# One RWKV and PReLU kernel: u loaded on its own queue, fills and the token table moved to GpSimd, the check of alpha moved back

## The chip, the cores and the metric

The kernel runs on one core of a Trainium2 chip. The core has five engines with an instruction stream each: TensorE (PE; its weight loads are shown as PEld), VectorE (DVE), ScalarE (ACT), GpSimd (POOL) and SyncE (SP, which issues most of the DMAs). They wait for one another by semaphores. The metric is the time of one execution on the device, in microseconds (us); less is better.

## The reference, cut to what matters

An attention-like recurrence for 4 batches, 8 heads, 768 tokens and a head size of 48, and behind it a two-layer network with a leaky activation whose slope `alpha` is a number for each of 2048 inner features:

```python
state = zeros(B, H, D, D)
for t in range(S):
    cur = einsum('bhd,bhe->bhde', u[None] * kt, vt)
    y[:, :, t] = einsum('bhd,bhde->bhe', rt, state + cur)
    state = w[None, :, :, None] * state + einsum('bhd,bhe->bhde', kt, vt)
x = y.transpose(0, 2, 1, 3).reshape(B * S, H * D)
h = x @ w_in                                   # (3072, 384) @ (384, 2048)
out = (maximum(h, 0) + alpha * minimum(h, 0)) @ w_out
```

All tensors are float32. The decay `w` lies between 0.85 and 0.95.

## The kernel before, in words

**Chunks and pairs.** The 768 tokens are cut into six chunks of 128. The recurrence is done chunk by chunk, two heads (a "pair") at a time: four pairs q = 0 to 3 in each chunk. Within a chunk the products of r and k (the scores), masked to earlier tokens, stand for the recurrence; r and k are first multiplied by powers of the decay from a table W[q] (a scan of w and a reciprocal, L275 and L278). What passes from a chunk to the next is a state T[q].

**The first chunk** (`first_chunk`). For each pair: two loads (r and k, 224 KB each), two products with the table on VectorE (L447), scores on TensorE (L457, in two PSUM banks), the diagonal term with u (product L533 on VectorE, sums L540 on TensorE, L464 for v times these sums), masks that keep the part above the diagonal (`below`; for the first of two banks by a predicated copy on VectorE, L477, and for the second by a copy on ScalarE, L471, and a select on GpSimd, L473), and y on TensorE (L485 and L489). y goes to SBUF by ScalarE (L504) in a coarse and a fine part, with a correction matmul between (L508); pairs 1 to 3 also take up a piece of pair 0's heads (L498). The state needs k by tokens times a table: `tokens_table` makes eight pieces of 112x64 (L315, two for each pair), transposes them on TensorE (L322), copies the result (`whalf`, L325), scales k with it (L431), and L521 makes the product.

**Chunks 1 to 5** (`prepare`, `burst`). The same in a denser form, at set steps of the network. Here the diagonal goes into the scores' mask itself: `base` holds for each of 2 heads and 4 batches a 64x64 identity times a sum `cu`, and VectorE copies the scores over its upper part (L681). In chunk 1 (called hasty) these eight fills for each pair are GpSimd operations (L594), later ones ScalarE copies (L598). TensorE's bursts are L626, L633, L652 and L662.

**The network** runs in 96 steps, 16 blocks of 128 inner features for each chunk: nine matmuls in (L740), the activation on ScalarE and VectorE (L748, L749, L752, L753), nine matmuls out (L774), some steps later. Weights come packed and are unpacked once into a coarse and a fine part, wh and wl, by ScalarE and VectorE (L359, L362, L365, L374, L377, L378).

**The check** (`check`, L813 to L829) counts whether all alpha are at most 1 and w is in a range; SyncE and the others read the flag and branch to a slow general path if not.

**What sets the order.** A planner (`Plan.in_order`) takes all pieces with an estimated duration, what they read and write, and a rank. It walks through time with its own estimates and gives each engine the ready piece of lowest rank. The engines then run their streams in that order, so a rank or an estimate that is changed moves instructions. Where the plan leaves TensorE idle before the first output matmul, filler matmuls on the identity are put in (`warm`, L834); 19 more stand at the start of the program. Loads are in the same order on SyncE's queue, the first r on ScalarE's (L420). Buffers and five PSUM banks are given out in the same walk.

## Time and profile before

| | |
|---|---|
| median of 3 runs | 485.31 us (484.8 to 485.47) |
| profiled execution | 485.77 us |
| its span, first to last instruction | 483.7 us |
| TensorE busy | 473.4 us (98%) |
| VectorE busy | 309.9 us (64%) |
| ScalarE busy | 244.8 us (51%) |
| GpSimd busy | 98.4 us (20%) |
| mean granted TensorE clock | 0.998 |

The shares are means over two stages. In the first 80 us the first two chunks and the unpacking of the weights run beside the first steps of the network, and VectorE and ScalarE are busy most of the time; after that the network's matmuls follow one another. Busy times of TensorE are those of pipelined matmuls, whose ends are modelled, so what one piece of work takes is better read from the start of its first matmul to the start of the next piece.

### The profile page before, as it was taken

To read this page: it belongs to the slowest core of one execution; us is meant where nothing else is said; L and a number is where in the kernel's file an instruction comes from. 1 tells how busy PE (TensorE), PEld (TensorE's weight loads), DVE (VectorE), ACT (ScalarE), POOL (GpSimd) and SP (SyncE) were. 2 spreads that over 40 slices of the span, in tenths; PEclk is the share of its full clock that TensorE was granted. 3 is DMA by queue.
4 is the path that set the end of the run, shared out by engine and by line. 5 is a ranking of instruction groups with operands and counts; after the bars stand their busy time and mean duration, and the time that the engine had idled before them with its cause. 6 is when DMAs were issued, how large, how long until landed. Compare 5 with 4: busy or idle time off the path is not lost.

```text
span 483.7 us, 11271 instructions
## 1 busy us (share of the span) xinstructions
PE 473.4 (98%) x4667; PEld 385.5 (80%) x4667; DVE 309.9 (64%) x519; ACT 244.8 (51%) x554; POOL 98.4 (20%) x119
## 2 busy tenths in 40 slices
PE   8999999999999999999999999999999999999994
PEld 6777777888888888888888888888888878888883
DVE  6999899999777774864754865754553543333330
ACT  3877897766555553553552653553642342423332
POOL 5119890012414030411201402200200000000000
PEclk9999999999999999999999999999999999999999
DMA  7975885641154631521211421210400000100002
GB/s 220 284 228 184 250 248 170 214 147 51 54 160 122 211 96 59 149 88 37 88 54 37 151 89 35 72 56 1 119 1 1 1 1 0 66 0 1 0 0 71
DMA packets 23113, 46.22 MB, mean 96 GB/s; under 512 B 3376, under 2 KB 11184, under 8 KB 23056
## 3 DMA queue, kind: packets, MB, share of 16 engines
q1 hardware_dynamic: 21968, 43.24, 28.5%
q0 software_dynamic: 960, 1.97, 2.0%
q8 instruction: 38, 0.62, 0.5%
q10 hardware_dynamic: 128, 0.23, 0.2%
q14 instruction: 19, 0.16, 0.1%
HBM read 37.17 MB, written 6.29 MB: 90 GB/s over the span
## 4 chain that ended last, share of the span: by engine, by line
PE 86%; DVE 5%; POOL 4%; ACT 2%; DMA 2%; issue 1%; ACTq 0%; DVEq 0%
PE acc L774 40%; PE bank L740 38%; POOL base L594 4%; PE bank L652 2%; PE bank L662 2%; PE bank L633 2%; PE bank L626 1%; DMA raw<-rk 1%; DVE raw L447 1%; ACT x L717 1%; DVE raw L565 1%; DMA wp<-wP 1%; DVE wl L378 1%; DVE kk L431 0%; DVE g L533 0%
## 5 line engine op out<-in xcount | busy, mean ns | idle before, releaser
L740 PE MATMUL bank<-x,wh 128*128 128x512 f32 x576 | 195.3, 392 | 0.0
L749 DVE SCALAR_TENSOR_TENSOR g<-bank,alph,g 128x512 f32<-128x512 f32 x96 | 71.9, 749 | 106.6 <-ACT g L748 106.5
L740 PEld LDWEIGHTS bank<-x,wh 128*128 128x128 f32 x576 | 108.1, 188 | 24.0 <-issue 0.8
L748 ACT ACTIVATE g<-bank 128x512 f32<-128x512 f32 x96 | 57.2, 596 | 129.2 <-PE bank L740 128.8
L740 PE MATMUL bank<-x,wl 128*128 128x512 f32 x288 | 112.2, 389 | 0.0
L752 ACT ACTIVATE gh<-g 128x512 fp32r<-128x512 f32 x96 | 60.5, 630 | 72.2 <-DVE g L749 72.1
L753 DVE TENSOR_TENSOR gl<-g,gh 128x512 fp32r<-128x512 f32 x96 | 72.4, 754 | 36.9 <-ACT gh L752 36.8
L774 PE MATMUL acc<-gh,wh 128*128 128x512 f32 x288 | 83.2, 396 | 0.0
L774 PE MATMUL acc<-gh,wl 128*128 128x512 f32 x288 | 81.6, 390 | 0.0
L774 PE MATMUL acc<-gl,wh 128*128 128x512 f32 x288 | 81.5, 390 | 0.0
L774 PEld LDWEIGHTS acc<-gh,wl 128*128 128x128 f32 x288 | 53.9, 188 | 11.4
L774 PEld LDWEIGHTS acc<-gl,wh 128*128 128x128 f32 x288 | 53.9, 188 | 11.3
L740 PEld LDWEIGHTS bank<-x,wl 128*128 128x128 f32 x288 | 54.1, 188 | 10.8
L774 PEld LDWEIGHTS acc<-gh,wh 128*128 128x128 f32 x288 | 52.7, 188 | 11.6 <-issue 0.4
L582 POOL TENSOR_TENSOR rr<-rr,kk 128x384 f32<-128x384 f32 x16 | 22.3, 1393 | 161.4 <-DMA kk<-vkr 93.6
L598 ACT ACTIVATE base<-ident,cu 128x64 f32<-128x64 f32 x128 | 32.9, 337 | 1.7 <-DVE cu L588 1.7
L594 POOL TENSOR_SCALAR base<-ident,cu 128x64 f32<-128x64 f32 x32 | 30.8, 984 | 13.7 <-ACT cu L546 13.7
L390 POOL DMA_DIRECT2D x<-x x30 | 15.4, 519 | 61.3 <-ACT o L801 49.4
L406 DVE TENSOR_TENSOR x<-bank,x 48x256 fp32r<-48x256 f32 x64 | 27.0, 422 | 1.3
L405 ACT ACTIVATE x<-bank 48x256 fp32r<-48x256 f32 x64 | 24.2, 379 | 2.1 <-PE bank L662 1.0
L568 DVE TENSOR_TENSOR raw<-raw,W 112x512 f32<-112x512 f32 x32 | 22.4, 723 | 2.2 <-DMA raw<-rk 2.2
L584 POOL TENSOR_TENSOR rr<-rr,utab 128x384 f32<-128x384 f32 x16 | 22.5, 1408 | 1.2
(116 smaller groups left out, 395.8 us busy)
## 6 DMA issues: line engine op xcount, KB each, us to landing
wraw<-wall SPq DMA_DIRECT2D x15, 768.0 KB, 4.7
raw<-rk SPq DMA_DIRECT2D x45, 224.0 KB, 3.9
v<-vkr SPq DMA_DIRECT2D x24, 192.0 KB, 3.4
kk<-vkr SPq DMA_DIRECT2D x20, 192.0 KB, 3.6
rr<-vkr SPq DMA_DIRECT2D x16, 192.0 KB, 2.5
oT<-o SPq DMA_DIRECT2D x12, 256.0 KB, 2.2
x<-x POOLq DMA_DIRECT2D x30, 64.0 KB, 2.7
oT<-g SPq DMA_DIRECT2D x6, 256.0 KB, 4.3
```

Of the source, the lines that this page charges most:

```text
L405: add("ACT", us, lambda: nc.scalar.activation(h(), view(), AF.Copy), r=[src], w=parts(x, 0, ps), rank=rank)
L406: add("DVE", us + 0.1, lambda: nc.vector.tensor_tensor(out=l(), in0=view(), in1=h(), op=ALU.subtract), r=[src] + parts(x, 0, ps), w=parts( ...
L568: add("DVE", 0.72, lambda t=t, tab=tab: nc.vector.tensor_tensor(out=t().rearrange("p b (j t) -> p (b j) t", j=2), in0=t().rearrange("p b ( ...
L584: add("POOL", 1.2, lambda: nc.gpsimd.tensor_tensor(out=rt().rearrange("p (g b) e -> p g b e", g=2), in0=rt().rearrange("p (g b) e -> p g b ...
L594: add("POOL", 1.0, lambda g=g, b=b: nc.gpsimd.tensor_scalar(base()[:, g, b], ident2(), cu()[:, g, b:b + 1], None, op0=ALU.mult), r=[cu, id ...
L598: add("ACT", 0.32, lambda g=g, b=b: nc.scalar.activation(base()[:, g, b], ident2(), AF.Copy, scale=cu()[:, g, b:b + 1]), r=[cu, ident2], w ...
L740: nc.tensor.matmul(hp()[:, :], a[i]()[:, k], X[c]()[:, x, k], start=(k == 0 and j == 0), stop=(k == NK - 1 and j == 2))
L748: add("ACT", 0.6, lambda: nc.scalar.activation(g(), hp()[:, :], AF.Copy), r=[hp], w=[g], rank=n - 100)
L749: add("DVE", 0.75, lambda: nc.vector.scalar_tensor_tensor(out=g(), in0=hp()[:, :], scalar=alph()[:, i:i + 1], in1=g(), op0=ALU.mult, op1=A ...
L752: add("ACT", 0.64, lambda: nc.scalar.activation(gh(), g(), AF.Copy), r=[g], w=[gh], rank=n - 100)
L753: add("DVE", 0.73, lambda: nc.vector.tensor_tensor(out=gl(), in0=g(), in1=gh(), op=ALU.subtract), r=[g, gh], w=[gl], rank=n - 99)
L774: nc.tensor.matmul(banks[k](), a[i]()[:, NK + k], x(), start=(begin and j == 0), stop=(end and j == 2))
```

## The change

Seven things are edited.

- u is loaded from ScalarE's queue, ahead of the first r, instead of from SyncE's; w stays first on SyncE's. The planner counts small loads with a fixed time.
- The four operations that square the last element of the table into `w128` (L279) go from VectorE to GpSimd.
- For pairs 0 and 1 of the first chunk both banks are masked by a ScalarE copy and a GpSimd select, where the first bank was a predicated copy on VectorE. The two memsets that those copies needed fall away, and the planner's estimate of a select goes from 1.6 to 0.75.
- The eight pieces of the token table (L315) go from ScalarE to GpSimd; the transposes behind them (L322) get a lower rank.
- The diagonal fills of all later chunks, eight small operations for each pair, on GpSimd in chunk 1 and on ScalarE afterwards, become two GpSimd selects of 64x512 that read `cu` with a step of zero.
- The check moves from step 40 to step 24, and two of its operations now also read the last weight tile, so they can't run before the weights are unpacked.
- 16 filler matmuls instead of 19 at the start, and none in the gap right behind them.

```diff
-                dma = max(dma, p.end + 1.5) + p.kb / DMA_RATE
-                p.end = dma + 0.3
+                if p.kb < 16:
+                    p.end += 1.7
+                else:
+                    dma = max(dma, p.end + 1.5) + p.kb / DMA_RATE
+                    p.end = dma + 0.3
...
-    load(up, lambda: nc.sync.dma_start(up(), uP), 1, -98.95)
+    add("ACT", 0.45, lambda: nc.scalar.dma_start(up(), uP), w=[up], rank=-111, kb=1)
...
-        for g in range(2):
-            if g == 0:
-                add("POOL", 0.4, lambda i=i, g=g: nc.gpsimd.memset(below[i][g](), 0.0), w=[below[i][g]], rank=-95 + i)
...
-        add("DVE", 0.1, lambda: nc.vector.tensor_tensor(
+        add("POOL", 0.25, lambda: nc.gpsimd.tensor_tensor(
             out=w128()[:, m:m + 1], in0=t()[:, 128:129], in1=t()[:, 128:129], op=ALU.mult), r=[t], w=[(w128, m)],
             rank=10 * m - 78)
...
-                add("ACT", 0.3, lambda m=m, j=j: nc.scalar.activation(
-                    rows()[:, m, HI * j:HI * (j + 1)], W[m]()[:, L - 1:HI - 1:-1], AF.Copy,
-                    scale=w128()[:, m:m + 1] if first and j == 0 else W[m]()[:, L:L + 1]),
+                add("POOL", 0.5, lambda m=m, j=j: nc.gpsimd.tensor_scalar(
+                    rows()[:, m, HI * j:HI * (j + 1)], W[m]()[:, L - 1:HI - 1:-1],
+                    w128()[:, m:m + 1] if first and j == 0 else W[m]()[:, L:L + 1], None, op0=ALU.mult),
                     r=[W[m], (w128, m)], w=[(rows, (m, j))], rank=at)
...
-        add("PE", 0.6, turn, r=[rows, ident], w=[pt], rank=at)
+        add("PE", 0.6, turn, r=[rows, ident], w=[pt], rank=at - 49 * first)
...
-            if g and True:
-                add("ACT", 0.6, lambda: nc.scalar.activation(
-                    base[1]().rearrange("p b t -> p (b t)"), A[1]()[:, :], AF.Copy), r=[A[1]], w=[base[1]], rank=q - 94)
-                add("POOL", 1.6, lambda: nc.gpsimd.affine_select(
-                    base[1](), base[1](), pattern=[[0, B], [1, L]], base=0, channel_multiplier=-1,
-                    compare_op=ALU.is_gt, fill=0.0), w=[base[1]], rank=q - 94)
+            if g or q < 2:
+                add("ACT", 0.6, lambda g=g: nc.scalar.activation(
+                    base[g]().rearrange("p b t -> p (b t)"), A[g]()[:, :], AF.Copy), r=[A[g]], w=[base[g]], rank=q - 94)
+                add("POOL", 0.75, lambda g=g: nc.gpsimd.affine_select(
+                    base[g](), base[g](), pattern=[[0, B], [1, L]], base=0, channel_multiplier=-1,
+                    compare_op=ALU.is_gt, fill=0.0), w=[base[g]], rank=q - 94)
                 continue
...
-        for g in range(2):
-            for b in range(B):
-                if hasty:
-                    add("POOL", 1.0, lambda g=g, b=b: nc.gpsimd.tensor_scalar(
-                        base()[:, g, b], ident2(), cu()[:, g, b:b + 1], None, op0=ALU.mult), r=[cu, ident2],
-                        w=[(base, (g, b))], rank=at - 0.9)
-                    continue
-                add("ACT", 0.32, lambda g=g, b=b: nc.scalar.activation(
-                    base()[:, g, b], ident2(), AF.Copy, scale=cu()[:, g, b:b + 1]), r=[cu, ident2],
-                    w=[(base, (g, b))], rank=at - 0.9)
+        for j in range(2):
+            rows = slice(HI * j, HI * (j + 1))
+            add("POOL", 0.75, lambda rows=rows: nc.gpsimd.affine_select(
+                base()[rows].rearrange("p g b t -> p (g b) t"),
+                cu()[rows].rearrange("p g b -> p (g b)")[:, :, None].broadcast_to([HI, 2 * B, HI]),
+                pattern=[[0, 2 * B], [1, HI]], base=0, channel_multiplier=-1, compare_op=ALU.is_equal, fill=0.0),
+                r=[cu], w=[base], rank=at - 0.9)
...
-        at = 40
+        at = 24
...
-        add("DVE", 0.1, lambda: nc.vector.tensor_scalar(ok()[:, 0:NF], alph(), 1.0, None, op0=ALU.is_le), r=[alph],
+        add("DVE", 0.1, lambda: nc.vector.tensor_scalar(ok()[:, 0:NF], alph(), 1.0, None, op0=ALU.is_le), r=[alph, wl[NF - 1]],
...
-    add("PE", 4.0, lambda: [warm() for _ in range(19)], r=[ident], w=[(bank, "warm")], rank=-1000)
+    add("PE", 3.4, lambda: [warm() for _ in range(16)], r=[ident], w=[(bank, "warm")], rank=-1000)
...
-    tokens_table(L, True, -45)
+    tokens_table(L, True, -44)
```

The order of the instructions moves in many places, of which three matter below. In it, line numbers of the changed kernel differ by a few from those before (L322 and L457 are the same in both, L740 is L737, L834 is L831).

**VectorE, its first operations behind the memsets.** `W_95`, `W_96` and `W_97` are the tables of pairs 0, 1 and 2, `raw` is r or k. Before:

```order
L275 SCALAR_TENSOR_TENSOR W_95<-wp,unit 112x65
L278 RECIPROCAL W_95<-W_95 112x64
L447 TENSOR_TENSOR raw<-raw,W_95 112x512 x2
L533 TENSOR_TENSOR g<-raw 112x512
L275 SCALAR_TENSOR_TENSOR W_96<-wp,unit 112x65
L278 RECIPROCAL W_96<-W_96 112x64
```

And in the changed kernel:

```order
L275 SCALAR_TENSOR_TENSOR W_95<-wp,unit 112x65
L278 RECIPROCAL W_95<-W_95 112x64
L275 SCALAR_TENSOR_TENSOR W_96<-wp,unit 112x65
L278 RECIPROCAL W_96<-W_96 112x64
L447 TENSOR_TENSOR raw<-raw,W_95 112x512
L275 SCALAR_TENSOR_TENSOR W_97<-wp,unit 112x65
L447 TENSOR_TENSOR raw<-raw,W_95 112x512
L533 TENSOR_TENSOR g<-raw 112x512
```

Pair 1's table and the scan of pair 2's now stand ahead of pair 0's second product.

**GpSimd, from u's products to chunk 1.** `below` and `gl` are the masked scores of even and odd pairs, `g` in L315 is the token table. Before:

```order
L270 TENSOR_TENSOR uw<-up,wp 48x4 x2
L473 AFFINE_SELECT below_136<-below_136 128x512
L473 AFFINE_SELECT gl<-gl 128x512
L473 AFFINE_SELECT below_136<-below_136 128x512
L473 AFFINE_SELECT gl<-gl 128x512
L594 TENSOR_SCALAR base<-ident_90,cu 128x64 x16
```

And in the changed kernel, from pair 1's selects on:

```order
L473 AFFINE_SELECT gl<-gl 128x512 x2
L315 TENSOR_SCALAR g<-W_95,w_99 112x64
L473 AFFINE_SELECT below_136<-below_136 128x512
L315 TENSOR_SCALAR g<-W_95 112x64
L315 TENSOR_SCALAR g<-W_96,w_99 112x64
L315 TENSOR_SCALAR g<-W_96 112x64
L315 TENSOR_SCALAR g<-W_97,w_99 112x64
L315 TENSOR_SCALAR g<-W_97 112x64
L473 AFFINE_SELECT gl<-gl 128x512
L315 TENSOR_SCALAR g<-W_98,w_99 112x64
L315 TENSOR_SCALAR g<-W_98 112x64
L593 AFFINE_SELECT base<-cu 64x512 x4
```

The eight pieces of the table stand among the selects of pairs 2 and 3, and the fills of chunk 1 are four instructions where 16 were.

**TensorE, around the token table's transpose.** Behind pair 2's y, whose bank is `bank_142` before and `bank_143` afterwards, there stood:

```order
L498 MATMUL bank_142<-x_338,pick 128x512 x2
L485 MATMUL bank_146<-ident,gh 128x128 x4
L489 MATMUL bank_146<-gl,v 48x128 x8
L498 MATMUL bank_146<-x_338,pick 128x512 x2
L508 MATMUL bank_142<-x,less_138 128x512
L322 MATMUL bank_144<-ident,g 128x112 x4
```

And now, from the correction of pair 1 (`bank_142`) on:

```order
L508 MATMUL bank_142<-x,less_138 128x512
L322 MATMUL bank_146<-ident,g 128x112 x4
L498 MATMUL bank_143<-x_345,pick 128x512 x2
L485 MATMUL bank_144<-ident,gh 128x128 x4
L489 MATMUL bank_144<-gl,v 48x128 x8
L508 MATMUL bank_143<-x,less_138 128x512
L498 MATMUL bank_144<-x_345,pick 128x512 x2
```

L322 now stands ahead of the rest of pairs 2 and 3.

## Rows read from the trace of the kernel before

**Rows 1.** Table by stretch: stretch, its us, busy us per engine (x), PEclk, DMA.

```profile
30.69:80.00 49.31, 48.05 (x771) 36.53 (x770) 45.18 (x72) 40.75 (x86) 37.84 (x40) 1.00 0.71 221
80.00:476.67 396.67, 396.66 (x3578) 327.36 (x3576) 238.01 (x393) 184.43 (x420) 53.06 (x54) 1.00 0.22 68
```

**Rows 2.** Timeline of TensorE, start: start us, us, instruction, [idle before <-releaser].

```profile
1.46 5.09 PE L834 MATMUL acc<-ident 128*128 128x256 bf16 x23 [1.46 <-POOL ident L249]
6.48 1.55 PE L457 MATMUL bank<-raw 48*128 48x128 f32 x16
...
8.52 0.83 PE L834 MATMUL acc<-ident 128*128 128x256 bf16 x6
9.28 1.16 PE L457 MATMUL acc<-raw 48*128 48x128 f32 x16
...
12.67 0.39 PE L834 MATMUL acc<-ident 128*128 128x256 bf16 x2
13.25 1.16 PE L457 MATMUL bank<-raw 48*128 48x128 f32 x16 [0.19 <-DVE raw L447]
```

**Rows 3.** Timeline of TensorE, 16.9 to 64 us.

```profile
16.92 0.73 PE L498 MATMUL bank<-x,pick 112*128 112x512 f32 x2
...
21.27 0.73 PE L498 MATMUL bank<-x,pick 112*128 112x512 f32 x2
...
25.15 0.39 PE L834 MATMUL acc<-ident 128*128 128x256 bf16 x2
25.69 0.60 PE L303 MATMUL bank<-ident,raw 112*128 112x112 f32 x4 [0.16 <-DVE raw L565]
...
30.69 0.82 PE L834 MATMUL acc<-ident 128*128 128x256 bf16 x6
31.50 0.67 PE L521 MATMUL bank<-v,kk 128*64 128x48 f32 x16
32.40 0.63 PE L540 MATMUL bank<-uw,g 112*64 112x2 f32 x16 [0.24 <-DVE g L533]
...
43.64 0.59 PE L652 MATMUL bank<-raw,T 48*48 48x64 f32 x26 [0.34 <-DVE base L681]
...
63.09 0.66 PE L652 MATMUL bank<-raw,T 48*48 48x64 f32 x32 [0.69 <-ACT x L717]
```

**Rows 4.** Timeline of VectorE, its first operations on the table.

```profile
3.73 0.29 DVE L275 TENSOR_TENSOR_SCAN W<-wp,unit 112x65 f32<-112x65 f32 x1 [2.60 <-DMA wp<-wP]
4.06 0.55 DVE L278 RECIPROCAL W<-W 112x64 f32<-112x64 f32 x1
4.64 1.32 DVE L447 TENSOR_TENSOR raw<-raw,W 112x512 f32<-112x512 f32 x2
```

**Rows 5.** DMA issues: queue, count, KB, us from issue to landing.

```profile
raw<-rk ACTq DMA_DIRECT2D x1, 224.0 KB, 3.3
```

**Rows 6.** Timeline of VectorE: a mask of the first chunk.

```profile
18.23 0.73 DVE L477 COPY_PREDICATED below<-strict,bank 128x512 f32<-128x512 uint8 x1
```

**Rows 7.** Line L594 on GpSimd; the timeline of GpSimd and VectorE beside its longest.

```profile
L594 POOL TENSOR_SCALAR base<-ident,cu x32: 433/442/4077, 34.0 to 66.1; 128x64 f32<-128x64 f32 x32
54.56 4.08 POOL L594 TENSOR_SCALAR base<-ident,cu 128x64 f32<-128x64 f32 x1
55.03 0.95 DVE L374 SCALAR_TENSOR_TENSOR wx<-wraw,wx 128x768 uint32<-128x768 uint32 x1
...
57.37 0.95 DVE L378 TENSOR_TENSOR wl<-wx,wh 128x768 fp32r<-128x768 f32 x1
```

**Rows 8.** Timeline of GpSimd and VectorE: a select, and the product beside it.

```profile
8.81 0.64 POOL L473 TENSOR_SCALAR_AFFINE_SELECT below<-below 128x512 f32<-128x512 f32 x1 [2.78 <-ACT below L471]
8.85 1.14 DVE L533 TENSOR_TENSOR g<-raw 112x512 f32<-112x512 f32 x1
...
13.23 0.69 DVE L533 TENSOR_TENSOR g<-raw 112x512 f32<-112x512 f32 x1
```

**Rows 9.** Table by stretch, TensorE alone, behind its last matmul.

```profile
476.70:481.70 5.00, 0.00 (x0) 1.00 0.46 166
```

More of the change, by code (lines that the diff above doesn't have):

```diff
@@ L811, in check @@
         count = psum()
-        at = 40
+        at = 24
         add("POOL", 0.1, lambda: (ok(), w2(), nc.gpsimd.memset(ok()[:, 0:NF + P], 0.0)), w=[ok], rank=at)
-        add("DVE", 0.1, lambda: nc.vector.tensor_scalar(ok()[:, 0:NF], alph(), 1.0, None, op0=ALU.is_le), r=[alph],
+        add("DVE", 0.1, lambda: nc.vector.tensor_scalar(ok()[:, 0:NF], alph(), 1.0, None, op0=ALU.is_le), r=[alph, wl[NF - 1]],
             w=[ok], rank=at)
-        add("DVE", 0.1, lambda: nc.vector.tensor_tensor(out=w2(), in0=wp(), in1=wp(), op=ALU.mult), r=[wp], w=[w2],
+        add("DVE", 0.1, lambda: nc.vector.tensor_tensor(out=w2(), in0=wp(), in1=wp(), op=ALU.mult), r=[wp, wl[NF - 1]], w=[w2],
             rank=at)
@@ L858, in rwkv_prelu_kernel @@
         jobs.append((n + MLAG - 0.5, 5, lambda n=n: m_out(n)))
-    jobs.append((40, 7, check))
+    jobs.append((24, 7, check))
     for m in range(P):
@@ L878, in rwkv_prelu_kernel @@
             step = p.rank >= 0 and p.us == 0.7
-            fill[p], last = 0 if last is None else int(max(0.0, p.start - last - 0.05) / (0.25 if step else 0.125)), p.end
+            fill[p] = 0 if last is None else int(max(0.0, p.start - last - 0.05) / (0.25 if step else 0.125))
+            last = p.end if p.rank > -1000 else None
     with tc.manual_schedule():
```

## The prediction

> **What bounds the kernel now.** I read the table of busy time by stretch first. From 80 us to the last matmul at 476.67 TensorE has 0.01 us without work, and between 30.69 and 80 it lacks 1.26 us (49.31 less 48.05) [rows 1]. The matmuls that count are the same ones in both programs: the listed order has every kind in the same number, and only the filler matmuls of L834 drop from 39 to 20. So from 80 us on nothing can be won, whatever the other engines do, and the time moves only by what TensorE wastes before. The next view is TensorE's timeline. The waste is, in order: 6.48 us until the first scores, of which 23 fillers fill 5; two fillers at 12.67 with an idle bit behind (0.58 us to the next piece) [rows 2]; two at 25.15 (0.54 to 25.69), six at 30.69 (0.81 to 31.50), and idle time of 0.24, 0.34 and 0.69 us before L540 and L652 [rows 3]. Behind the start that is 3.2 us together. It is the whole prize, under 0.7%, and it is also all the cover: a new wait of TensorE in this stage is paid in full.
>
> **The change, part by part.** The profiled execution took 485.77 us, 2.07 more than its span of 483.7; the median of the runs is 485.31. I work out a difference in the profiled execution and put it on the median.
>
> *The start.* The first scores (L457) wait for r and k of pair 0 times the table. Before, VectorE needed a scan, a reciprocal and two products, 3.73 to 5.96 [rows 4]. In the new order pair 1's scan and reciprocal (0.29 and 0.55) and pair 2's scan stand in between: 5.45 for the first product, 7.0 for the end of the second, so scores start near 7.05 against 6.48. The load of r goes behind u on ScalarE's queue: issued some 0.45 us later it lands near 4.5 (issued at 0.80, it took 3.3 us before [rows 5]) and is needed at 5.45, so it costs nothing; a landing a whole microsecond later still would be paid here. The 0.6 comes back at once: the two fillers at 12.67 are gone, and pair 1's products, which end at 9.4 instead of 8.8, find TensorE among four fillers. Where pair 1's y (L489) ends, 16.92 before, I put the new kernel at 17.05: **+0.1**.
>
> *Work moved off VectorE and ScalarE.* Two masks (0.73 each [rows 6]), four tiny products and four small operations of alpha's check leave VectorE's order here; eight small copies leave ScalarE and two larger ones come. TensorE waits for neither between 16.92 and 30.69, where its pieces follow one another and only the fillers stand between. I price it at nothing; what hides it is TensorE's own work.
>
> *Work moved onto GpSimd.* The token table's eight pieces (L315) become GpSimd operations, and L322, the transpose that reads all eight, is moved ahead in TensorE's order: behind it there now stand L498 of pair 2, all of pair 3's y, the corrections and the state products. What does such an operation cost on GpSimd? The nearest row is L594, the same operation on 128x64: 433 ns at least, 442 at the median, 4077 at most. The long one shows why: it begins at 54.56 and ends at 58.64, 0.3 us behind a run of four VectorE operations with two SBUF operands each that stand without a gap, 55.03 to 58.32 [rows 7]. In the other direction, the select that begins at 8.81 keeps its 0.64 us, and VectorE's product at 8.85 takes 1.14, against 0.69 for the next pair's at 13.23 [rows 8]. So the two engines shut each other out, and where VectorE's row has no gap, GpSimd stands.
>
> The Trainium skill states this as a lock ("SBUF — State Buffer", section "SBUF: two separate sides"): of a VectorE operation with two SBUF inputs and a GpSimd operation that reads SBUF, whichever starts first has the shared ports to its end. The rows agree, in both directions. Its page "Perfetto Trace Analysis", section "Optimizing Scalar/DVE Operations", speaks against the change: moving work between these two engines might not help.
>
> Now by hand along VectorE's new order. From pair 2 on: two products and a diagonal product (0.65 each from start to start; closed to GpSimd), the v product that reads PSUM (0.46; open), the same for pair 3 (closed, 13.7 to 15.7), v product and mask (open, to 17.3), two half-tile steps of the weights (L365, L374, 0.47 each; closed, to 18.3), mask and v product (open, to 19.4), four half-tile steps (closed, to 21.4). VectorE's next operation is then L325, which waits for L322 itself: open. GpSimd from 15.7 on: piece 1 of the table, a select, piece 2; from 18.3 pieces 3 and 4; from 21.4 pieces 5 and 6, the last select, pieces 7 and 8, at 0.42 and 0.6 each, 2.3 us. The table is ready at about **23.6**. TensorE comes to L322 after six pieces, L457, L540, L498, L485, L489 and L508; the same six filled 16.92 to 21.27 before, 4.35 us [rows 3]. 17.05 and 4.35 is 21.4: it waits 2.2 us. Of the stretch 16.92 to 30.69, 13.77 us, there remain behind L322, without the fillers (0.54) and these six, 8.88. 23.6 and 8.88 is 32.48, where the old kernel stood at 30.69: **+1.8**.
>
> *After that.* The six fillers (0.81) and the wait for L533 (0.24) go: in the new order six matmuls of the next step stand before that L540, and its product is done some 2 us earlier than TensorE comes. **-1.05**. The diagonal fills of chunk 1, 32 operations of L594, become eight selects of 0.64 (two for eight operations that took about 8 us), so VectorE's L681 is not kept by them; the waits of 0.34 and 0.69 at L652 may go, or others take their place, since VectorE stays busy for 45.2 of 49.3 us [rows 1]. Between nothing and 1.03 I take half: **-0.5**.
>
> *Later chunks* lose 128 copies on ScalarE and get 32 selects on GpSimd. From 80 us on TensorE waits for neither, and two selects of 0.64 are no longer than eight copies. If a burst did come late, it would be 0.3 to 0.7 us each, as at L652. Alpha's flag, and SyncE's wait for it, move from 42 us to step 24; the loads behind it have several microseconds to spare there. Zero for both.
>
> Sum (the 0.1 is inside the 1.8): 1.8 less 1.05 less 0.5 is +0.25, and the least sure of these, VectorE's remaining waits, I leave at half. On the median: **485.5 us**, which is no change.
>
> **The rivals.** *GpSimd is in time.* If GpSimd wins its races, as the select at 8.81 did, each piece of the table takes 0.42 and each select 0.6; the last select waits for pair 3's copy (done 18.8), and the table is ready at 20.3, a microsecond before TensorE comes. L322 costs nothing: 17.05 and 13.23 (13.77 less 0.54) is 30.28, -0.4, and with -1.05 and -0.5 the kernel gains 1.95: 483.4 us. For it speaks that GpSimd could begin the table as early as 14; against it, the 16 operations of L594 between 34 and 50 us, which took a microsecond each. By the Trainium skill's lock this is the case where GpSimd is first each time.
>
> *GpSimd is later still.* With a microsecond for each of the ten operations left at 15.7, the table is ready at 25.7, L322 holds everything for 4.3 us, 25.7 and 8.88 is 34.6, +3.9, and with -1.05 and -0.5 the kernel ends +2.35: 487.7. It decides from an L322 at 24.3 on, where the sum passes +1. For it: L594's usual microsecond; against it, that VectorE itself runs dry at 21.4 and lets GpSimd go.
>
> *The clock rises late.* The fillers at the start stand 0.22 us apart (23 in 5.02), those at 8.52 some 0.12 (six in 0.76) [rows 2]: the level of 1.2 GHz first, that of 2.4 after. The granted clock is still 1.00 through 5 us without a matmul at the end [rows 9], so a wait of 2 us should not lower it; but the new kernel's 16 fillers stop near 4.9 and scores start at 7.05. If its pieces then stand at the lower level for as long as the first ones did (1.46 to 6.48 at least; say until 12.9), they take twice as long there, up to 2.9 us more. Most of that is lost in the wait at L322: TensorE would come there at 24.3 instead of 21.4, 0.7 behind the table. +0.7 on the forecast, 486.2: still no change.
>
> *The change does nothing*, since all that it touches lies beside TensorE's work: 485.3, on the forecast's side.
>
> **How the numbers follow.** Forecast, with the late clock and the no-effect case: 0.44. GpSimd in time: 0.32. GpSimd later, or a wait as long elsewhere: 0.24. The range: lowest, L322 free and both waits gone, -2.5, so 482.8; highest, GpSimd later and neither wait gone, +2.85, so 488.2, cut a little since it needs both. I take 482.9 to 488.0; the likeliest case alone spans 484.4 to 486.3. About 0.2%, or 0.97 us, is what a measurement can tell from no change, so faster 0.32, same 0.44, slower 0.24.
>
> **What would show it.** In the profile after: first scores near 7.05; L315 on GpSimd at 0.42 us in VectorE's gaps and a microsecond or more where it has none; idle time of some 2 us before L322, released by GpSimd, with the table ready at 23.6; the first L740 near 29.6; no L834 behind 10 us; no idle time before L540. Wrong would be no wait at L322 (faster), or a first L740 later than 31 us (slower).

## The result, and the profile after

The changed kernel took 493.06 us (median of 4 runs, 491.94 to 502.47) against 485.39 (484.8 to 485.91) for the kernel before beside it: a ratio of 1.0147, 95% interval 1.0126 to 1.0167. It is slower by 1.5%, 7.6 us above the 485.5 of the forecast. The intervals here leave out executions more than 1.5% above the fastest of their kernel, the medians hold all. The first profiled execution was the slowest one (502.47 us, span 500.3), so the same program was run and profiled again (the run `again` below: 491.57 us, span 489.5).

Busy time by stretch of the first profile, cut where the granted clock changes (columns: stretch, its length, busy time and instructions of PE, PEld, DVE, ACT, POOL, granted clock, DMA share, GB/s):

```profile
0.00:8.38 8.38, 4.62 (x32) 3.22 (x32) 4.24 (x11) 3.26 (x16) 4.65 (x22) 1.00 0.73 209
8.38:32.27 23.89, 23.89 (x192) 19.20 (x189) 14.67 (x26) 10.07 (x19) 10.10 (x15) 0.50 0.68 216
32.27:144.91 112.64, 107.21 (x1240) 84.07 (x1240) 103.56 (x149) 72.10 (x138) 33.35 (x34) 1.00 0.50 155
144.91:151.74 6.83, 6.16 (x44) 4.76 (x36) 4.47 (x11) 3.20 (x9) 1.95 (x2) 0.50 0.86 278
151.74:496.48 344.74, 342.42 (x3160) 282.44 (x3159) 186.40 (x319) 123.69 (x237) 62.10 (x70) 1.00 0.19 58
```

For 24 us, from 8.38 to 32.27, TensorE ran at 0.50 (1.2 GHz), and once more for 6.83 us from 144.91. The full level (1.00, 2.4 GHz) is on record from 4.96 on; the view counts the time before that as 1.00, though the first fillers stand 0.22 us apart. The second profile, of the same instructions:

```profile
7.14:15.76 8.62, 8.62 (x90) 7.03 (x92) 8.48 (x15) 2.26 (x5) 5.46 (x6) 0.60 1.06 336
15.76:80.00 64.24, 63.20 (x963) 48.12 (x964) 57.65 (x89) 53.42 (x109) 17.31 (x24) 1.00 0.73 223
80.00:476.67 396.67, 392.77 (x3557) 323.36 (x3556) 240.11 (x400) 149.95 (x283) 87.06 (x92) 1.00 0.22 67
```

Here the clock is full from 5.52 to 8.94, the low level ends at 15.76, and one thing stands in both that the kernel before did not have [rows 1]: behind 80 us TensorE is idle, 3.90 us (396.67 less 392.77) against 0.01. What it waited for in the second profile (engine, tile, line, what released it: us in total, times, longest):

```profile
PE bank L457 <- DVE raw L447: 2.1, 1, 2.1
PE bank L322 <- POOL g L315: 1.6, 2, 1.3
PE bank L649 <- DVE g L746: 1.5, 1, 1.5
PE acc L831 <- POOL ident L252: 1.5, 1, 1.5
PE bank L659 <- ACT seen_y L672: 0.8, 1, 0.8
PE bank L540 <- DVE g L746: 0.6, 1, 0.6
```

L457 and L831 (the fillers) are at the start, L540 is at 60 us; L322, L649 and L659 lie behind 80 us. Since the 1728 matmuls of the network come in the same number in every kernel, the start of the n-th of them can be set against that of the kernel before. This ledger (us later than before, worked out from each profile's TensorE instructions; the column heads give the time in the kernel before) is what the rest rests on:

| profile | at 81 us | at 98 us, behind the second table | at 124 us | at 134 us, behind a burst of chunk 2 | at 425 us |
|---|---|---|---|---|---|
| changed, first profile | 9.55 | 11.48 | 11.48 | 16.63 | 17.51 |
| `again` | 0.54 | 2.46 | 2.46 | 5.64 | 6.05 |
| `more_fill` | 0.23 | 0.91 | 1.74 | 5.86 | 6.21 |
| `chk_more` | 0.78 | 1.45 | 2.27 | 5.54 | 5.87 |
| `base_more` | -0.08 | 0.86 | 0.86 | 3.04 | 3.40 |
| `base_chk_more` | 0.27 | 2.40 | 2.40 | 2.40 | 2.42 |
| `base_chk_own_more` | 1.57 | 1.11 | 1.11 | 1.71 | 1.74 |
| `start_only` | 2.10 | 2.11 | 2.11 | 2.10 | 2.11 |
| `b_base` | 0.77 | 0.77 | 0.77 | 4.34 | 4.31 |
| `b_few` | -0.41 | -0.41 | -0.41 | -0.41 | -0.38 |

So in the second profile the changed kernel is only half a microsecond behind at 81 us, where I had it 0.25 behind. It loses 1.9 us at the second token table and 3.2 at one burst of chunk 2, where I had zero: 5.1 of the 6.05 that it is behind at 425 us. The medians (492.8 and 493.06) lie 1.2 and 1.5 us above this execution (491.57); in which stage, no profile shows.

### The profile page after: what moved, and what is told of

Its sections match the earlier page's. It is cut to its first block, busy times and chain, and to the rows that moved or that the text cites. A ratio compares the mean times of both kernels' runs of the same rounds, so it can differ in the third digit from the quotient of the medians.

```text
span 500.3 us, 11128 instructions
## 1 busy us (share of the span) xinstructions
PE 484.3 (97%) x4648; PEld 393.7 (79%) x4648; DVE 313.3 (63%) x513; ACT 212.3 (42%) x416; POOL 112.1 (22%) x143
## 4 chain that ended last, share of the span: by engine, by line
PE 85%; DVE 6%; DMA 3%; ACT 2%; issue 2%; POOL 1%; ACTq 0%; POOLq 0%
PE acc L771 36%; PE bank L737 35%; PE bank L649 2%; PE bank L659 2%; DMA wraw<-wall 2%; PE bank L630 2%; PE bank L489 1%; PE bank L623 1%; DVE gl L750 1%; DVE wl L378 1%; DMA raw<-rk 1%; DVE g L746 1%; PE acc L457 1%; PE acc L540 1%; DVE wx L374 1%
## 5 line engine op out<-in xcount | busy, mean ns | idle before, releaser
L737 PE MATMUL bank<-x,wh 128*128 128x512 f32 x576 | 195.4, 392 | 0.0
L746 DVE SCALAR_TENSOR_TENSOR g<-bank,alph,g 128x512 f32<-128x512 f32 x96 | 72.0, 749 | 108.8 <-ACT g L745 107.4
L737 PEld LDWEIGHTS bank<-x,wh 128*128 128x128 f32 x576 | 108.6, 188 | 24.0 <-issue 1.2
L737 PE MATMUL bank<-x,wl 128*128 128x512 f32 x288 | 112.4, 390 | 0.0
L750 DVE TENSOR_TENSOR gl<-g,gh 128x512 fp32r<-128x512 f32 x96 | 73.3, 763 | 36.9 <-ACT gh L749 36.5
L749 ACT ACTIVATE gh<-g 128x512 fp32r<-128x512 f32 x96 | 60.5, 630 | 72.3 <-DVE g L746 72.3
L771 PE MATMUL acc<-gh,wh 128*128 128x512 f32 x288 | 84.4, 400 | 0.0
L593 POOL TENSOR_SCALAR_AFFINE_SELECT base<-cu 64x512 f32<-64x512 f32 x40 | 36.7, 918 | 157.4 <-PE bank L659 120.4
L737 PEld LDWEIGHTS bank<-x,wl 128*128 128x128 f32 x288 | 54.2, 188 | 10.9
L582 POOL TENSOR_TENSOR rr<-rr,kk 128x384 f32<-128x384 f32 x16 | 20.3, 1271 | 33.1 <-DMA kk<-vkr 21.3
L584 POOL TENSOR_TENSOR rr<-rr,utab 128x384 f32<-128x384 f32 x16 | 21.2, 1326 | 1.2
L659 PE MATMUL bank<-base,v 64*48 64x64 f32 x640 | 17.6, 219 | 2.3 <-ACT seen_y L672 2.3
```

Of the source, the lines that this page charges most:

```text
L584: add("POOL", 1.2, lambda: nc.gpsimd.tensor_tensor(out=rt().rearrange("p (g b) e -> p g b e", g=2), in0=rt().rearrange("p (g b) e -> p g b ...
L593: add("POOL", 0.75, lambda rows=rows: nc.gpsimd.affine_select(base()[rows].rearrange("p g b t -> p (g b) t"), cu()[rows].rearrange("p g b ...
L659: nc.tensor.matmul(where(g, b, j), v0()[s, g * B + b], base0()[s, g, b], start=False, stop=(crossed == 1 and e == 0), skip_group_check=True)
L737: nc.tensor.matmul(hp()[:, :], a[i]()[:, k], X[c]()[:, x, k], start=(k == 0 and j == 0), stop=(k == NK - 1 and j == 2))
L746: add("DVE", 0.75, lambda: nc.vector.scalar_tensor_tensor(out=g(), in0=hp()[:, :], scalar=alph()[:, i:i + 1], in1=g(), op0=ALU.mult, op1=A ...
L749: add("ACT", 0.64, lambda: nc.scalar.activation(gh(), g(), AF.Copy), r=[g], w=[gh], rank=n - 100)
```

## The experiments

Sixteen kernels ran with three timed rounds each beside the kernel before (its medians: 484.7 to 485.04).

**The program again, and more fillers.**

> The changed kernel as it is, once more. In the profiled execution (502.47 us) the granted clock fell at 8.38 us, behind 2.29 us in which TensorE waited for the first products, and came back at 32.27; other executions of the same program took 491.9 to 493.2 us with a mean clock of 0.987 to 0.998. Theory 'clock': the low level in the first stage is the main cause, in each execution to a different extent; then a run at 492 should still show a stretch at 0.5 behind 8 us, and the first L737 some 5 us later than the first L740 before (26.06). Theory 'waits': at 492 the clock is at 1.00 from about 8 us on, and the 6.5 us lost stand as idle time of TensorE: about 2 before the first scores or L322, 2.3 at the second L322 (104 us in the profiled run), and 2 to 3 around the bursts of chunk 1 (L649, L659).

492.8 us (491.57 to 496.1). The waits behind 80 us are there at the full clock, and the low level lasts to 15.76. How it comes (TensorE; start, us, engine, line, idle time before it and its releaser):

```profile
1.47 3.60 PE L831 MATMUL acc<-ident 128*128 128x256 bf16 x16 [1.47 <-POOL ident L252]
7.14 1.16 PE L457 MATMUL bank<-raw 48*128 48x128 f32 x16 [2.08 <-DVE raw L447]
```

```diff
-    add("PE", 3.4, lambda: [warm() for _ in range(16)], r=[ident], w=[(bank, "warm")], rank=-1000)
+    add("PE", 3.4, lambda: [warm() for _ in range(32)], r=[ident], w=[(bank, "warm")], rank=-1000)
```

> The changed kernel with 32 filler matmuls at the start instead of 16, the planner's estimate and so the order of everything else untouched; at 0.22 us each for those at the low level and 0.12 at the high one they reach to about 7 us, when the first scores start at 7.36. Theory 'clock': the granted clock no longer falls at 8.38, pieces from 7 to 32 us run at the full pace, the time falls to 485 to 488 us and executions near 500 disappear. Theory 'waits': executions near 500 disappear, but the median stays at 491 to 493, since the waits behind 25 us stay.

491.78 us (491.45 to 492.55), 1.0139 [1.0118, 1.0161]. The spread shrinks from 10.5 us (the changed kernel's first four runs) to 1.1, and the granted clock is 1.00 in a stretch where its mean was 0.60 above, a row of the same view:

```profile
7.10:15.76 8.66, 7.84 (x122) 6.39 (x123) 8.56 (x14) 3.67 (x7) 4.86 (x7) 1.00 1.06 331
```

The first matmul of the network stands at 27.77 us instead of 29.39. But by 134 us that is gone: the median moves by 1 us only. Both theories hold a part each; the late clock explains the spread and about 1 us of the median, not the rest of the loss.

**Fewer fillers in the kernel before.**

```diff
-    add("PE", 4.0, lambda: [warm() for _ in range(19)], r=[ident], w=[(bank, "warm")], rank=-1000)
+    add("PE", 4.0, lambda: [warm() for _ in range(12)], r=[ident], w=[(bank, "warm")], rank=-1000)
```

> The kernel before with 16 filler matmuls ahead of the first scores instead of 23, as the changed kernel has them; the planner's estimates and the order of everything else stay. TensorE then has nothing to do from about 5.1 to 6.48 us. In the profiles so far the granted clock is at its full level for good from 7.32 us (before, 23 fillers, no gap), 4.15 (the changed kernel with 32 fillers, gap 0.67), but only from 15.76, 15.85, 16.95, 17.43, 22.13, 30.32 and 32.27 where 16 fillers are followed by a gap of 1.84 to 2.33 us. Theory 'clock': the same happens here, the full level comes for good at 15 us or later, the pieces from 6.5 to 16 us take up to twice as long, and since no other wait of that stage hides it the time rises by 2 to 5 us, to 487 to 490. Theory 'waits': the number of fillers changes nothing, 484.7 to 485.7.

Ten executions, in us: 484.33, 484.43, 484.86, 485.97, 486.2, 488.7, 488.82, 489.08, 493.83, 494.51; 17 of the kernel before beside them lay within 484.38 to 486.36. The two slowest had a mean granted clock of 0.972 and 0.973, the others 0.996 to 0.999. In the profiled one (484.33) the scores start at 5.72, sooner than before, since they no longer stand behind fillers, and the clock stayed up. So the seven fillers cost 0.4 us in a good execution; without them, half of the executions took some 4 to 10 us longer. The `clock` theory has the median right (487.45), but that lies between two groups of executions, and the profiled one shows no late clock. For the three executions near 489 the late clock is not shown: their mean clock is 0.998, and a first rise that comes late does not show in that mean (it was 0.997 in the profile of `base_back` below, with the first full level at 16.95 us).

**Parts undone one at a time, at 16 fillers.** Six kernels: the first token table and the second on ScalarE again (`tok_back`), the fills (`base_back`), the check (`chk_back`), the second table alone on ScalarE (`tab2act`), and the second table left on GpSimd with a buffer of its own, alone (`tab_own`) and with the check back (`tab_own_chk`).

```diff
 tok_back
-                add("POOL", 0.5, lambda m=m, j=j: nc.gpsimd.tensor_scalar(
+                add("ACT", 0.3, lambda m=m, j=j: nc.scalar.activation(
...
-        add("PE", 0.6, turn, r=[rows, ident], w=[pt], rank=at - 49 * first)
+        add("PE", 0.6, turn, r=[rows, ident], w=[pt], rank=at)
 base_back
-        for j in range(2):
...
+        for g in range(2):
+            for b in range(B):
+                if hasty:
...
 chk_back
-        at = 24
+        at = 40
 tab2act
+                if first:
                     add("POOL", 0.5, lambda m=m, j=j: nc.gpsimd.tensor_scalar(
...
+                    continue
+                add("ACT", 0.3, lambda m=m, j=j: nc.scalar.activation(
 tab_own
-        rows, pt = sb([112, P, L], "g", 3), psum()
+        rows, pt = sb([112, P, L], "g", 3) if first else sb([112, P, HI], "tab", 1), psum()
```

> The changed kernel with the token table as before: its pieces (L315) on ScalarE, and the first transposes (L322) at their old place in TensorE's order. Theory 'clock': no effect beyond 1 us, 491 to 493. Theory 'waits on GpSimd': the 2.3 us at the second L322 and what stands before the first one go, 487 to 489. A third possibility is that the planner's other choices carry the loss; then it stays within 1 us of 492 although no wait stands at L322.

> The changed kernel with the diagonal fills as before (L594 and L598 again, 160 small operations on GpSimd in chunk 1 and on ScalarE later, instead of 40 selects). Theory 'waits on GpSimd', this part of it: the selects take 0.92 us in the mean where 0.64 was reckoned, so bursts wait for them; without them the time falls by 1 to 3 us, to 489 to 491. If the fills are not the cause it stays at 492 within 1 us; ScalarE then has about 35 us of work more and its waits may grow.

> The changed kernel with the check of alpha back at step 40 and without its tie to the last weight tile. In the profile of the changed kernel at 489.5 us, TensorE loses 3.2 us at the burst of chunk 2 (L649 and L659, 132.6 to 137.4): VectorE's L746 stands behind L431, which waits for GpSimd's L582, which waits for a load (L580) that was issued at 129.57, behind L588 at 129.0; the check's four VectorE operations (126.2 to 127.9, 1.1 us) stand ahead of that L588. Theory 'check': without them L588 and the load come 1 us or more earlier, the two waits shrink, and with the check's later cost (0.35) the time falls by 2 to 3.5 us, to 489 to 490.5. Theory 'GpSimd queue': the chain was late before the check came (loads at 104.1, 113.7, 122.1 against 102.9, 109.9, 118.0), so at most 1 us is won, 491.5 to 492.5.

> The changed kernel with the pieces of the second token table in a buffer of its own, still on GpSimd. In the changed kernel these pieces write a g buffer that comes free at 92.8 us, and GpSimd has nothing done from 64.7 to 92.9 while the product L582 of chunk 2 stands behind them (69.2 before, 96.7 after). Theory 'GpSimd queue': with the own buffer the pieces run early, no wait at the second L322 (2.25 us won), and the chain of chunk 2 starts near 70 us again, so that part of the 3.2 us at 132 to 137 goes too: 487 to 489.5. Theory 'check' or 'VectorE's order': only the 2.25 us are won, 489.5 to 490.5. If the wait at L322 stays, both are wrong.

> The changed kernel with only the second token table back on ScalarE, the first one stays on GpSimd. Theory 'GpSimd queue': as with the own buffer, no wait at the second L322 and L582 of chunk 2 near 70 us: 487 to 490. Since the planner moves other work with it, a loss of 1 to 3 us may also stand elsewhere before 80 us; then it says that the order as such, not one part, carries the loss there.

> The changed kernel with both: the second table in its own buffer and the check at step 40. If the two waits have these two causes and nothing else, what both win adds up: no idle time of TensorE over 0.3 us behind 85 us, and 485 to 487 us, the time at which my prediction stood. If VectorE's order of chunk 2 (L588 some 4 us behind the end of L584) is the cause whatever stands ahead, 1.5 to 3 us at L649 and L659 remain: 488 to 490.

Medians, in this order: 494.76, 497.55, 493.85, 496.77, 495.83 and 495.52 us, all above that of the changed kernel (`chk_back` by less than its spread) and all with spreads of 2.4 to 5.7 us. As times these six miss: with 16 fillers the late clock (in their profiles the full level came at 15.85 to 30.32 us) hides what was to be measured. Their ledgers still tell two things. Wherever the second table is off the network's buffers or off GpSimd, nothing is lost at it (`tok_back` 6.37 at 81 and at 98 us, `tab_own` 8.95 and 8.95, `tab2act` 4.48 and 4.48; `chk_back` 2.17 and 4.10, `base_back` 4.20 and 5.16). And none of them frees the burst: 3.1 us are lost between 124 and 134 us in `tok_back`, 3.3 in `tab_own`, 2.6 in `tab_own_chk`, 2.4 in `chk_back`, 2.0 in `base_back`, 6.0 in `tab2act` (where the clock fell once more). At the second table other kernels that keep it as it is lose 0.7 to 2.1 us (table above). The theory that GpSimd's long wait makes the chain of chunk 2 late falls: in `tab_own_chk` the first L582 stood at 66.8 us and the loss stayed.

The wait at the second table, in the second profile of the changed kernel, GpSimd and then TensorE:

```profile
92.89 3.81 POOL L315 TENSOR_SCALAR g<-W 112x64 f32<-112x64 f32 x4 [28.19 <-DVE gl L750]
96.66 1.01 POOL L582 TENSOR_TENSOR rr<-rr,kk 128x384 f32<-128x384 f32 x1
```

```profile
94.54 0.36 PE L322 MATMUL bank<-ident,g 112*64 112x112 f32 x2
95.16 0.29 PE L322 MATMUL bank<-ident,g 112*64 112x112 f32 x1 [0.26 <-POOL g L315]
96.75 0.29 PE L322 MATMUL bank<-ident,g 112*64 112x112 f32 x1 [1.31 <-POOL g L315]
```

The four pieces write a buffer that the network gives free only at 92.9; GpSimd does nothing for 28.19 us until then, and takes 3.81 us for four operations that need 0.44 each when it is alone, beside VectorE's L369, L371 and L750. TensorE waits between the pieces.

**Two parts undone together, then with a steady clock.** `base_chk` has the fills and the check back; `base_chk_more` adds the 32 fillers, `base_chk_own_more` also the second table's own buffer. The edits are those above.

> The changed kernel with two parts undone: the diagonal fills as before (L594, L598) and the check at step 40. Of one part alone neither moved the loss at the burst of chunk 2 much (2.0 us with the fills back, 2.4 with the check back, 3.2 with none). Theory 'each lengthens the chain': the chain load, L582, L584, L588 goes round once for each pair of chunk 2 with a single buffer; in the changed kernel its rounds take 9.6, 8.4 and 7.5 us, with the fills back 7.1, 7.6 and 8.4 (the last with the check's four operations inside), before 7.1, 8.0 and 7.6. Then with both undone the rounds are near 7.1, 7.6 and 7.5, no wait over 0.4 us at L649 or L659, and 488.5 to 490.5 us (the slow start and the second L322 remain). Rival, 'the order of the rest': 1.5 us or more remain there and it stays at 491.5 to 493.

> As the last, and with 32 fillers at the start. Theory 'clock' with 'chain': what the late clock costs at the start (1.6 to 3 us) is won as well, and is not taken back at the burst as it was when only fillers were added: 486 to 488 us, and the executions lie within 1.5 us of one another. If the burst takes it back again the chain is still the bound: 489 to 490.

> As the last, and with the second token table in a buffer of its own. All of the causes named so far are then taken away (late clock, chain of chunk 2, second L322), while u's load, the masks, the first token table and w^128 stay changed: 484.5 to 486 us if nothing else costs. What it is above 485 is the price of the rest in the first 80 us.

493.51 us (489.42 to 497.78), 487.56 (487.04 to 488.38; 1.0045 [1.0026, 1.0064]) and 487.09 (486.44 to 488.72; 1.0051 [1.0035, 1.0067]). In `base_chk` two of the four executions lie where they were expected (489.42 and 489.94), the other two at 497. With both parts back only 0.52 us are lost between 124 and 134 us in `base_chk`, behind the burst, and none in `base_chk_more`. But not for the expected reason: the rounds did not go back to 7.1, 7.6 and 7.5 us but took 8.4, 7.8 and 6.5, and in `base_chk_more` the load that ends the loop is issued at 129.61, as late as in the changed kernel (129.57). What differs is VectorE's order, told below. The fillers then take 6 us off the median, and 2.4 off the fastest execution. The own buffer takes the loss at the second table away (2.13 to -0.46), but its planner's order loses 1.3 us more before 81 us and 0.6 at the burst, and the median stays 1.1 us above the 484.5 to 486 that I expected. TensorE's waits in `base_chk_more`:

```profile
PE bank L322 <- POOL g L315: 1.6, 1, 1.6
PE acc L834 <- POOL ident L252: 1.5, 1, 1.5
PE bank L508 <- ACT x L504: 1.1, 1, 1.1
```

**Fills and check told apart.** `chk_more` and `base_more` are `chk_back` and `base_back` with the 32 fillers; `b_base` is the kernel before with nothing but the change's edit of the fills (eight operations of L594 or L598 for a pair become two selects).

> The changed kernel with 32 fillers at the start and the check at step 40; the fills stay GpSimd selects. With the start steady the two suspects of the chain of chunk 2 can be told apart. Theory 'selects': GpSimd's selects and VectorE's operations beside them stretch one another (in the changed kernel VectorE's L374, L750 and L369 beside them took 1.29, 1.51 and 1.37 us, against 0.95, 0.69 and 0.55 elsewhere), so rounds of 9.6 and 8.4 us remain, 2 to 3 us are lost at L649 and L659, and the time is 490 to 491.5 us. Theory 'check': it was the check's operations, the loss there is under 1 us, and the time is 488 to 489.

> The changed kernel with 32 fillers and the fills as before (L594, L598); the check stays at step 24. Theory 'selects': rounds of 7.1 and 7.6 us are back, and only the check's 1.1 us stand in the last one: at most 1.2 us lost at L652 and L662, 488 to 489.5 us. Theory 'check': 2 us or more lost there, 489.5 to 491.

> The kernel before with one part of the change alone: the diagonal fills as GpSimd selects (L593). Its fillers stay at 23, so the clock should be full at 7.3 us as before. Theory 'selects': they lengthen the rounds of chunk 2 by 1 to 2.5 us each, where VectorE had 0.2 us to spare ahead of the burst at 129.85, so 2 to 3 us are lost there and the time is 486.5 to 488. If the selects cost nothing by themselves (as I predicted) it is 484.5 to 485.5.

With 32 fillers: check back alone 491.83 us (491.03 to 492.22), as `more_fill`; fills back alone 489.3 (488.65 to 492.43), 2.5 us less; both 487.56. `chk_more` comes near the theory `selects` (3.3 us lost at the burst). `base_more` fits neither: its time lies in the range of `selects`, but 2.2 us are lost at the burst, which only `check` allowed. So these two do not share the loss out: the planner's order of VectorE, which both theories left out, changes from kernel to kernel as well. `chk_more` and, with the fills back, `base_more`:

```profile
PE bank L649 <- DVE g L746: 1.9, 1, 1.9
PE bank L659 <- ACT seen_y L672: 1.7, 2, 0.9
```

```profile
PE acc L774 <- ACT gh L752: 1.1, 1, 1.1
PE bank L652 <- DVE g L749: 0.8, 1, 0.8
PE bank L662 <- ACT seen_y L675: 0.8, 1, 0.8
```

The kernel before with the selects alone took 490.67 us (489.53 to 491.83; 1.0122 [1.0097, 1.0147]), worse than either theory said: 0.77 us by 81 us and 3.57 at the burst. There GpSimd and VectorE read, from the same stretch:

```profile
103.77 6.19 POOL L593 TENSOR_SCALAR_AFFINE_SELECT base<-cu 64x512 f32<-64x512 f32 x2 [31.47 <-DVE cu L588]
110.04 1.02 POOL L582 TENSOR_TENSOR rr<-rr,kk 128x384 f32<-128x384 f32 x1
```

```profile
103.55 0.95 DVE L371 SCALAR_TENSOR_TENSOR wx<-wraw,wx 128x768 uint32<-128x768 uint32 x1
104.42 0.68 DVE L750 TENSOR_TENSOR gl<-g,gh 128x512 fp32r<-128x512 f32 x1
105.02 0.95 DVE L374 SCALAR_TENSOR_TENSOR wx<-wraw,wx 128x768 uint32<-128x768 uint32 x1
...
108.75 0.68 DVE L750 TENSOR_TENSOR gl<-g,gh 128x512 fp32r<-128x512 f32 x1
112.18 0.55 DVE L588 TENSOR_REDUCE cu<-rr 128x8 f32<-128x384 f32 x1 [2.75 <-POOL rr L584]
```

VectorE keeps its usual times and two selects take 6.19 us, where two need 1.4 to 1.9 in later chunks; L582 waits behind them, and VectorE's L588 then waits 2.75 us for GpSimd. In the changed kernel it came out the other way round:

```profile
105.69 1.29 DVE L374 SCALAR_TENSOR_TENSOR wx<-wraw,wx 128x768 uint32<-128x768 uint32 x1
106.90 1.51 DVE L750 TENSOR_TENSOR gl<-g,gh 128x512 fp32r<-128x512 f32 x1
108.34 1.37 DVE L369 TENSOR_SCALAR wx<-wx 128x768 uint32<-128x768 uint32 x1
...
113.09 0.54 DVE L588 TENSOR_REDUCE cu<-rr 128x8 f32<-128x384 f32 x1
```

Here it is L374 (beside the selects, 104.19 to 106.17), L750 and L369 (beside L582 and L584) that are stretched, from 0.95, 0.68 and 0.55, and L588 comes 9.6 us behind the one before it, with no gap in VectorE's row. Whichever engine wins, this round of the loop is 2 us longer than before (7.05). The rule of the Trainium skill that the prediction cites ("SBUF — State Buffer", section "SBUF: two separate sides": who starts first has the shared ports to its end) agrees with the stretched L374 and L750, which have two SBUF inputs; L369 has one, and no run here shows why it is stretched.

**What is left of the change.** Both tables on ScalarE, fills and check as before, 32 fillers.

> The changed kernel with everything undone that cost something in the runs so far: both token tables on ScalarE, fills and check as before, 32 fillers; what stays are u on ScalarE's queue, the masks of pairs 0 and 1, w^128 on GpSimd and the planner's estimates. If these gain what the prediction's first part took them to gain (fillers 0.81 and 0.24 us of waits, less 0.6 at the start), 484 to 485 us; if the planner's new order costs more than that, 485.5 to 487.5.

487.42 us (486.86 to 487.52; 1.0049 [1.0032, 1.0066]): slower too. The ledger has 2.10 us, all before 81 us. 0.58 is the later start (scores at 7.06 against 6.48), and nearly all the rest is one wait in the planner's new order:

```profile
80.99 0.96 PE L774 MATMUL acc<-gh,wh 128*128 128x512 f32 x3 [1.46 <-ACT gh L752]
```

No version beat the kernel before.

## Why the prediction was wrong

**The step that failed** is the first paragraph's "from 80 us on nothing can be won" read as nothing can be lost, and the term "later chunks: zero". It was mis-sized by 5.1 us: 1.9 at the second token table and 3.2 at the burst of chunk 2. TensorE waited for nothing there [rows 1], which holds for the order that the kernel had; the new plan has another order, and I followed it only in the first chunk.

At the burst two things come together. The first is a loop through SyncE, GpSimd and VectorE (the chain of the expectations), since the buffer `rr` is there once: load (L580, 2.3 us to land), two products on GpSimd (L582, L584, 1 us or more each), the sum on VectorE (L588), next load. L431 writes over what L582 reads and so waits for it. A round took 7 to 8 us before; in the changed kernel three rounds took 9.6, 8.4 and 7.5 us, and the last load ahead of the burst was issued at 129.57 instead of 125.58.

The second is VectorE's order. In the kernel before, VectorE and TensorE ahead of the burst:

```profile
127.52 0.74 DVE L749 SCALAR_TENSOR_TENSOR g<-bank,alph,g 128x512 f32<-128x512 f32 x1
129.11 0.56 DVE L431 TENSOR_TENSOR kk<-kk,whalf 128x384 f32<-128x384 f32 x1 [0.84 <-POOL rr L582]
```

```profile
129.85 0.66 PE L652 MATMUL bank<-raw,T 48*48 48x64 f32 x32
```

L749 frees a bank that the burst writes, and stands ahead of L431, which waits for the loop. In the changed kernel the same operation, L746, stands behind L431. VectorE is idle for 1.57 us before L431, though what L746 needs from ScalarE is there at 131.35:

```profile
130.77 0.58 ACT L745 ACTIVATE g<-bank 128x512 f32<-128x512 f32 x1
```

```profile
133.17 0.56 DVE L431 TENSOR_TENSOR kk<-kk,whalf 128x384 f32<-128x384 f32 x1 [1.57 <-POOL rr L582]
133.64 0.74 DVE L746 SCALAR_TENSOR_TENSOR g<-bank,alph,g 128x512 f32<-128x512 f32 x1
```

```profile
134.44 0.59 PE L649 MATMUL bank<-raw,T 48*48 48x64 f32 x26 [1.52 <-DVE g L746]
137.07 0.44 PE L659 MATMUL bank<-base,v 64*48 64x64 f32 x16 [0.82 <-ACT seen_y L672]
```

The burst does not read what this L431 makes (that k belongs to a later pair), so the 0.2 us that I saw to spare in the expectation of `b_base`, from L431's end at 129.67 to 129.85, were no slack of the burst. `base_chk_more` shows it. Its loop is as late as the changed kernel's, but its plan has L749 ahead of L431, and its burst starts 1.2 us before L431 and waits for nothing:

```profile
130.44 0.74 DVE L749 SCALAR_TENSOR_TENSOR g<-bank,alph,g 128x512 f32<-128x512 f32 x1
131.88 0.69 DVE L753 TENSOR_TENSOR gl<-g,gh 128x512 fp32r<-128x512 f32 x1 [0.70 <-ACT gh L752]
133.46 0.56 DVE L431 TENSOR_TENSOR kk<-kk,whalf 128x384 f32<-128x384 f32 x1 [0.89 <-POOL rr L582]
```

```profile
132.25 0.66 PE L652 MATMUL bank<-raw,T 48*48 48x64 f32 x32
```

It is the same in every profile. Where the operation that frees the bank is ahead of L431, 0 to 0.52 us are lost between 124 and 134 us (the kernel before, `b_few`, `base_chk`, `base_chk_more`, `start_only`); where it is behind, 0.6 to 6.0 (all others). How late the loop is then sets the size: with the last load issued 5.2 us ahead of the burst 0.60 is lost (`base_chk_own_more`), with 3.8 us 2.18 (`base_more`), with 3.0 us 3.18 (`again`) and 4.12 (`more_fill`). The edit of the fills alone makes both, the other order and the longer round (`b_base`). What stays open is the share of each: no kernel had the selects with the old order. My reckoning that two selects of 0.64 "are no longer than eight copies" compared durations. It left out that GpSimd and VectorE shut each other out, which the same text argues for the first chunk, while these copies had been on ScalarE, and that the edit makes a new plan.

**The second token table** was not priced at all. `tokens_table` is called twice; I followed L315 and L322 only in the first chunk. It cost 1.9 us, and with the table off GpSimd or off the network's buffers nothing (`tok_back`, `tab2act`, `tab_own`).

**L322 waits 2.2 us** (the term of +1.8) was wrong. In `more_fill`, where the clock is full, GpSimd and TensorE read

```profile
19.98 0.44 POOL L315 TENSOR_SCALAR g<-W,w 112x64 f32<-112x64 f32 x1
20.39 1.00 POOL L315 TENSOR_SCALAR g<-W 112x64 f32<-112x64 f32 x1
```

```profile
21.35 0.55 PE L322 MATMUL bank<-ident,g 112*128 112x112 f32 x4
```

TensorE comes at 21.35 (21.4 in the prediction) and the table is done at 21.39, not 23.6: the rival "GpSimd is in time", whose 20.3 was nearer. "No wait at L322" was also named as the sign of a faster kernel; it came, and the kernel was slower, since the loss stood where no sign was looked for. And the first L737 of `again`, 29.39 against the 29.6 foretold, is there by the low clock and not by this wait.

**The clock rises late** was among the rivals, at no more than 2.9 us and to 12.9 us, and folded into the forecast because the wait at L322 was to hide it. That wait was not there. In the second and the first profile the clock had been full from 5.52 and 4.96 us on and fell behind the gap, at 8.94 and 8.38; the low level lasted to 15.76 and 32.27: 1.6 us of the 29.39 against 27.77 in the one, 9.2 (37.00 against 27.77) in the other. The reason I gave against it, that the clock stays up for 5 us without a matmul at the end [rows 9], was read off an engine that had been busy for 470 us and carried over to one that had just begun; why it did not hold here is not shown.

**-1.05 and -0.5.** The six fillers and the old wait of 0.24 did go, but at 59 us TensorE waits 1.05 at L540 and at 65 us 0.58 at L659 in `more_fill`. That the sum at 81 us is 0.23 there, as forecast, is luck: two errors that cancel, +1.8 that did not come and a gain of 1.55 that did not come either.

**What held:** no filler behind 10 us, and that the whole prize was small. The scores came at 7.05 as foretold (7.10 in `more_fill`, 7.14 in `again`, 7.36 in the first profile), but not for the reason given. The load of r, now behind u on ScalarE's queue, took 4.3 us to land and not 3.3, and VectorE, done with both tables at 4.30, waited for it:

```profile
5.61 0.69 DVE L447 TENSOR_TENSOR raw<-raw,W 112x512 f32<-112x512 f32 x1 [1.31 <-DMA raw<-rk]
```

So the 0.6 us at the start were paid for this load, which the prediction let cost nothing, and hardly for pair 1's table.

**Alpha's flag** cost nothing by its wait, but its two matmuls (L820), which stood in the first chunk before, now stand among the network's: 0.34 us in the ledger of `again`, where they come at 156 us, 0.33 in `chk_more`, where they come at 230 us.

## What to carry to other kernels

A wait of zero holds for the order in which it was measured. When an edit makes a new plan, compare the order of every engine in every stage: find the operation that frees what a burst needs, and look at what now stands ahead of it, for whatever that one waits for, the burst waits for as well. Look for loops with a single buffer, where each added microsecond is paid once a round. Filler matmuls that look like waste can be what keeps the clock up; take them out only if the real work starts where they end, and judge by ten executions, not by the best (`b_few`). When a helper is moved to another engine, price each of its calls.

## What the runs showed of the hardware

- The granted clock after the fillers: 23 of them with no gap before the scores, full for good from 7.32 us (the kernel before) and 5.58 (`b_base`); 32 with a gap of 0 to 0.8, from 4.15 to 6.83 us in six profiles; 16 with a gap of 1.84 to 2.33, from 15.76 to 32.27 in nine. In five of these nine it had been full from 4.96 to 5.67 us on and fell between 8.38 and 9.08. With 16 and a gap of 0.67 (`b_few`) it was full from 5.57 in the profiled execution, and the time was anything from 484.33 to 494.51.
- It can fall late too: in the first profile of the changed kernel to 0.50 from 144.91 to 151.74, behind a wait of TensorE of 1.53 us at the burst that ended at 143.39, in `tab2act` from 138.19 to 145.01, behind one of 2.60, and in `tok_back` from 72.05 to 75.46, with no wait over 0.66 us in the 10 us before. Between 124 and 425 us the ledger of the first profile loses 2.4 us more than that of `again`.
- Two 64x512 selects on GpSimd took 1.37 us at their best, and 6.19 beside a row of VectorE operations without a gap, most of them with two SBUF operands.
- An operation of VectorE that waits holds up all that stand behind it in its order: L746 of the second profile, whose input was there at 131.35, started at 133.64, behind L431, and TensorE waited 1.52 us for it.
